# Attention and expert kernel: a head's output and logits in one tile, scratch rows stored by heads, output rows copied from scratch

## The chip, the cores and the metric

One NeuronCore of a Trainium2 chip runs the whole program. The metric is the device time of one execution in microseconds. Engines are named as the profile names them: PE is TensorE's matrix product, PEld its weight load, DVE VectorE, ACT ScalarE, POOL GpSimd and SP SyncE, which computes nothing here and issues nearly all DMAs.

## What is computed

Linear attention over 8 batches of 8 heads, 576 tokens of 64 features, then a mixture of 8 experts over all 4,608 tokens, of which each takes at most one.

```python
def phi(x):
    proj = np.einsum('bhsd,df->bhsf', x, w_phi)                 # 64 -> 128
    proj = proj - np.max(np.abs(proj), axis=-1, keepdims=True)
    return np.concatenate([np.exp(proj), np.exp(-proj)], axis=-1)
kv = np.einsum('bhsf,bhsd->bhfd', k_p, v);  z = np.sum(k_p, axis=2)
x = einsum(q_p, kv) / (einsum(q_p, z) + 1e-06)                  # one row of 512 per token
do_compute = x @ w_skip > 0;  out = x.copy()
logits = x @ w_gate                                             # 8 experts
e_idx = argmax(logits);  gate_w = softmax(logits)[e_idx]
out[do_compute] = x + gate_w * (np.maximum(x @ w1[e], 0.0) @ w2[e])
```

## The kernel before

**Attention.** The work runs in steps. A unit is four heads of one batch, for keys or for queries (16 units of each kind), and has 5 parts: four of 512 rows each (two heads by half of the tokens) and one, part 0, for the last 64 tokens of all heads. Each step takes one part of a key unit and one of a query unit through the stages: load (`st_load`, L287), transpose on VectorE (`st_t`, L324 and L322), projection on PE and two full passes on VectorE (`st_proj`, L347, L354, L357), exponentials on ScalarE, for queries after a transpose on PE (`st_exp_k`, `st_exp_q`, L393), sums on GpSimd (L380) and the attention products on PE (`st_use_k`, L415; `st_use_q`, L513, for the tails L492). The matrix that queries are multiplied by is extended beforehand (L446), so that one product gives 64 output columns, 9 partial logits (8 experts and the skip score) and the denominator: 74 columns a head, four heads or head parts to a PSUM bank.

`norm` (L460) empties that bank on VectorE: denominator (L464), reciprocal (L468), the product for the 64 output columns (L475, into `xm`, or `xt` for the tails of two batches) and the product for the 9 logits (L476, into `lgm` or `lgt`). It runs 72 times: 64 full parts and 8 tails.

`post(b)` (L541) follows a batch's last part: it sums the logits over heads (L568), finds the expert of each token, forms the gate value (`gate`, L592 and L590 write it and the token's number into two columns behind the second half of `xm`), counts places within the experts (`rank`, with masks on GpSimd in L637 and, for batches 0 to 5, four mask instructions in L646 that feed the products of L657), and stores. Three kinds of stores leave on SP's queue: `store_half` (L531, L533) puts the first four heads' columns into `xrows`, a scratch array in DRAM with rows of 514 numbers; `store_rows` (L596, L598) puts the second half with the two extra columns there; `rest` (L668, L673) writes both halves from SBUF to `out`.

**Experts.** After the picks of the first experts (`pick`, L685, `pick_third`) weights stream in by SP in chunks of 512 KB (L184, L187), ScalarE and VectorE or GpSimd split each into a high and a low part (L195, L200), GpSimd gathers token rows from `xrows` by index (L213), PE multiplies (L942 to L961), and GpSimd scatters finished rows over `out` (L889).

**What sets the order.** Every engine runs its own queue in order. From step 8 to 79 the order of PE and ScalarE is the one written in the program; the order of VectorE, GpSimd and SP, and all orders outside those steps up to the experts, is planned when the program is built, from modelled durations and dependences. In the expert part the order is written by hand. Steps in which pieces of `post` are due are given in `later` (gate 2 steps after the batch, `store_rows` 4, `rank` 4, the index products 7, `rest` 7). The last batch does gate and `store_rows` at once; its `rest` is called once eight weight chunks have been asked for (L1206). SP's queue is in order, so a DMA that waits holds the ones behind it.

Of the kernel before, what the change touches and what calls it, by code (L numbers as in the profile page):

```python
# [8 lines left out]
F32 = mybir.dt.float32  # L9
# [9 lines left out]
P = 128  # L19
# [5 lines left out]
def kernel(  # L25
# [17 lines left out]
    SQ = S  # L43
# [76 lines left out]
    const.tile([1, 64], I32, name="spare")  # L120
    mark = const.tile([1, 32], I32, name="mark")[:, 0:1]

    ft = const.tile([P, NSL, 4], I32, name="ft")
# [132 lines left out]
    with actx:  # L256
# [200 lines left out]
                )  # L457
            kva_of[u.g] = kva

        def norm(o, xdst, ldst, shape):  # L460

            den = small.tile([P, 4], F32, tag="den", name="den")
            rec = small.tile([P, 4], F32, tag="rec", name="rec")
            nc.vector.tensor_scalar(  # L464
                out=den.rearrange("p (t o) -> p t o", o=1), in0=o[:, :, NA1:NAUG],
                scalar1=1e-6, scalar2=None, op0=ALU.add,
            )
            nc.vector.reciprocal(out=rec, in_=den)  # L468
            rv = rec.rearrange("p (t o) -> p t o", o=1)
            a, c = shape  # L470

            def sh(x):
                return x.rearrange("p (a c) d -> p a c d", a=a)

            nc.vector.tensor_tensor(out=xdst, in0=sh(o[:, :, 0:D]), in1=sh(rv.broadcast_to([P, 4, D])), op=ALU.mult)  # L475
            nc.vector.tensor_tensor(  # L476
                out=ldst, in0=sh(o[:, :, D:NA1]), in1=sh(rv.broadcast_to([P, 4, NA1 - D])), op=ALU.mult)

        def st_use_q(u, i):
            if i == 0 and u.b % 2 == 0:  # L480
# [4 lines left out]
            if i == 0:  # L485

                for h in range(4):
                    pr, hd = h // 2, h % 2
                    for half in range(2):
                        for par in range(2):  # L490
                            g = u.g - NQ * (1 - par)
                            nc.tensor.matmul(  # L492
                                ov[par * 64:par * 64 + 64, h, :],
                                et_of[g][:, half, hd * P + pr * 64:hd * P + pr * 64 + 64], kva_of[g][:, half, h, :],
                                start=(half == 0), stop=(half == 1),
                            )
                if u.hq == 0:
                    xt_of[u.b // 2] = (
                        [xp.tile([P, 1, 4 * D + 2 * h], F32, tag="xt%d" % h, name="xt") for h in range(2)],
                        xp.tile([P, 1, H, E + 1], F32, tag="lgt", name="lgt"),  # L500
                    )
                xt, lgt = xt_of[u.b // 2]
                norm(ov, xt[u.hq][:, 0, 0:4 * D].rearrange("p (h a d) -> p a h d", h=2, d=D),
                     lgt[:, 0, u.hq * 4:(u.hq + 1) * 4, :].rearrange("p (a h) e -> p a h e", a=2), (2, 2))
# [3 lines left out]
            h0 = u.hq * 4 + 2 * pr  # L508
            for j in range(2):
                for hd in range(2):  # L510
                    for half in range(2):
# [4 lines left out]
                                start=(half == 0), stop=(half == 1),  # L516
                            )
            if u.hq == 0 and i == 1:
                xm_of[u.b] = (
                    [xp.tile([P, 4, 4 * D + 2 * h], F32, tag="xm%d" % h, name="xm") for h in range(2)],  # L520
                    xp.tile([P, 4, H, E + 1], F32, tag="lgm", name="lgm"),
                )
            xm, lgm = xm_of[u.b]
            norm(ov, xm[u.hq][:, 2 * th:2 * th + 2, 0:4 * D].rearrange(
                "p a (h r d) -> p a r h d", h=2, d=D)[:, :, pr],
                 lgm[:, 2 * th:2 * th + 2, h0:h0 + 2, :], (2, 2))
            if i == 4:
                c = slice(0, 4 * D)
# [12 lines left out]
        def post(b):  # L541
            last = b == B - 1
            xs, lgm = xm_of[b]
            xm = xs[1]
            t0 = 9 * (b // 2) + 4 * (b % 2)
            parts = [(xm, lgm, 0, 4)]
            if b % 2 == 1:
                xts, lgt = xt_of[b // 2]
                xt = xts[1]
                parts.append((xt, lgt, 4, 1))  # L550
            nt = 4 if b % 2 == 0 else 5
            T = slice(t0, t0 + nt)

# [13 lines left out]
            for xx, lg, o, n in reversed(parts):  # L567
# [17 lines left out]
            def gate():  # L585
                nc.scalar.activation(out=ex[:, 0:nt], in_=d[:, 0:nt], func=AF.Exp)
                nc.vector.tensor_reduce(out=ss[:, 0:nt], in_=ex[:, 0:nt], axis=AX.X, op=ALU.add)
                nc.vector.tensor_scalar(out=gt[:, 0:nt], in0=ss[:, 0:nt], scalar1=1e-9, scalar2=None, op0=ALU.add)
                for xx, lg, o, n in parts:
                    nc.scalar.activation(  # L590
                        out=xx[:, :, 4 * D + 1:4 * D + 2], in_=sid[:, t0 + o:t0 + o + n].rearrange("p (t o) -> p t o", o=1), func=AF.Copy)
                    nc.vector.reciprocal(out=xx[:, :, 4 * D:4 * D + 1], in_=gt[:, o:o + n].rearrange("p (t o) -> p t o", o=1))  # L592
# [17 lines left out]
            def rank():  # L610
# [31 lines left out]
                    count()  # L642
                if b > EB:
                    return
                for s in range(S):
                    nc.vector.scalar_tensor_tensor(  # L646
                        out=rm4[:, 0:nt, :, s], in0=bc(RKH[:, T], nt, E), scalar=float(s), in1=OH[:, T, :],
                        op0=ALU.is_equal, op1=ALU.mult,
                    )

            def index():
                if b > EB:
# [22 lines left out]
            if last:  # L675
                rests.extend((rank, rest))
# [627 lines left out]
```

## Time and profile before

| | us |
|---|---|
| median of 3 runs | 604.68 |
| lowest, highest | 603.16, 605.82 |
| profiled execution | 607.32 |
| its span, first to last instruction | 605.4 |
| busy in the span: PE | 561.3 |
| PEld | 469.8 |
| VectorE | 498.1 |
| ScalarE | 329.0 |
| GpSimd | 375.4 |

The profile is of one execution, a little slower than the median. An engine's busy time is the union of its instructions' times; PE's is modelled where matmuls overlap, so a busy PE may still not be at its peak. The average over the span mixes stages with different limits: attention runs to about 345 us, the experts from there on. The DMA engines moved 108.33 MB, a mean of 179 GB/s, in 250,233 packets, 192,417 of them under 512 bytes.

### The profile page before, as it was taken

The numbers are of one execution on the slowest core, as the hardware profiler recorded it, in microseconds if no ns is written. First come the engines' busy times: TensorE is split into PE (matmuls) and PEld (weight loads), VectorE is DVE, ScalarE is ACT, GpSimd is POOL, SyncE is SP. The second block draws the span as 40 slices with busy tenths as digits, with TensorE's granted clock in tenths as the row PEclk, the third lists the DMA queues.
The fourth block names the chain that finished last, engine by engine and source line by source line (L and its number), as shares of the span: only waits on it lengthen the run. The fifth ranks groups of instructions, "written<-read, shape, count | busy, mean of one in ns | idle before, by whom it ended". The sixth has DMA issues, their size and how long they took to land. (4 is left out here: it accounts for less than half of the span.)

```text
span 605.4 us, 18715 instructions
## 1 busy us (share of the span) xinstructions
PE 561.3 (93%) x7486; PEld 469.8 (78%) x7486; DVE 498.1 (82%) x1085; ACT 329.0 (54%) x649; POOL 375.4 (62%) x399
## 2 busy tenths in 40 slices
PE   4699999999999999999789799899999998999993
PEld 2477887777877788777667799798998987988892
DVE  5779998999989999899898749866789887867841
ACT  3266665665556555565453544345658665656720
POOL 5465567586675866848665635995567674638021
PEclk9799999999999999999899899899999999999997
DMA  9898898876778657521335297489787688777500
GB/s 158 155 156 166 190 196 181 189 135 138 164 160 189 124 142 180 121 74 46 106 106 184 71 300 268 155 289 310 202 284 227 232 288 297 244 224 261 193 20 30
DMA packets 250233, 108.33 MB, mean 179 GB/s; under 512 B 192417, under 2 KB 235553, under 8 KB 250144
## 3 DMA queue, kind: packets, MB, share of 16 engines
q1 hardware_dynamic: 245632, 97.58, 61.7%
q0 software_dynamic: 3200, 9.45, 4.3%
q8 instruction: 60, 0.98, 0.7%
q10 hardware_dynamic: 1312, 0.08, 0.1%
q14 instruction: 29, 0.24, 0.1%
HBM read 83.86 MB, written 24.02 MB: 178 GB/s over the span
## 5 line engine op out<-in xcount | busy, mean ns | idle before, releaser
L380 POOL TENSOR_TENSOR z<-ek 128x512 f32<-128x512 f32 x64 | 81.1, 1274 | 83.1 <-ACT ek L373 66.0
L200 POOL TENSOR_TENSOR w<-wraw_c,w 128x256 fp32r<-128x256 f32 x108 | 98.8, 947 | 49.6 <-ACT w L195 49.5
L195 ACT ACTIVATE w<-wraw_c 128x1024 fp32r<-128x1024 f32 x96 | 97.8, 1051 | 5.8 <-DMA wraw_c<-in_moe_w_dram 5.8
L200 DVE TENSOR_TENSOR w<-wraw_c,w 128x1024 fp32r<-128x1024 f32 x69 | 91.7, 1344 | 9.4 <-ACT w L195 8.2
L354 DVE TENSOR_REDUCE m<-ps_P 128x8 f32<-128x1024 f32 (+2 forms) x86 | 88.7, 1032 | 2.8 <-PE ps_P L347 2.8
L357 DVE TENSOR_TENSOR u<-ps_P,m 128x1024 f32<-128x1024 f32 (+2 forms) x86 | 88.5, 1029 | 2.3
L347 PE MATMUL ps_P<-wsrc,xT 64*64 64x128 f32 x2048 | 75.2, 283 | 14.2 <-DVE u L357 7.3
L513 PEld LDWEIGHTS ps_O<-kva,eq 128*64 128x64 f32 x2048 | 74.6, 138 | 16.3 <-DVE cs L703 4.7
L513 PE MATMUL ps_O<-kva,eq 128*64 128x74 f32 x2048 | 77.6, 230 | 6.7 <-DVE cs L703 4.1
L399 ACT ACTIVATE eq<-ps_U 128x512 f32<-128x512 f32 x64 | 38.2, 596 | 83.5 <-PE ps_U L393 82.5
L347 PEld LDWEIGHTS ps_P<-wsrc,xT 64*64 64x64 f32 x2048 | 59.5, 138 | 25.8 <-issue 14.7
L415 PE MATMUL ps_K<-ek,v 128*64 128x256 f32 x512 | 70.3, 394 | 0.0
L889 POOL DMA_INDIRECT out_dram<-o,si x22 | 32.4, 1474 | 57.1 <-DVE si L888 50.5
L956 PE MATMUL ps_O<-w,hh 128*128 128x512 f32 x160 | 64.2, 401 | 0.5 <-DVE o L903 0.5
L637 POOL TENSOR_SCALAR OP<-iota_p,rkp,wcol 128x128 bf16<-128x128 f32 x62 | 48.6, 795 | 13.4 <-DVE rec L468 7.2
L324 DVE STREAM_TRANSPOSE xT<-raw 128x512 f32<-128x512 f32 x64 | 43.9, 697 | 8.6 <-PE ps_P L347 4.5
L393 PE MATMUL ps_U<-ident,u 128*128 128x128 f32 x288 | 49.7, 291 | 0.3 <-DVE den L464 0.3
L372 ACT ACTIVATE ek<-u 128x512 f32<-128x512 f32 x64 | 41.0, 641 | 16.5 <-DVE u L357 9.7
L960 PE MATMUL ps_O<-w,hh 128*128 128x512 f32 x120 | 47.4, 395 | 0.1
L961 PE MATMUL ps_O<-w,hlo 128*128 128x512 f32 x120 | 47.3, 394 | 0.0
L415 PEld LDWEIGHTS ps_K<-ek,v 128*64 128x64 f32 x512 | 33.5, 139 | 16.5 <-issue 7.1
L386 POOL TENSOR_TENSOR z<-z,ekt 64x512 f32<-64x512 f32 x32 | 40.8, 1275 | 5.2 <-DMA xg<-xrows,idg 2.9
(254 smaller groups left out, 1203.6 us busy)
## 6 DMA issues: line engine op xcount, KB each, us to landing
wraw_c<-in_moe_w_dram SPq DMA_DIRECT2D x96, 512.0 KB, 5.3
raw<-in_k_dram SPq DMA_DIRECT2D x64, 144.0 KB, 3.2
raw<-in_q_dram SPq DMA_DIRECT2D x64, 144.0 KB, 3.6
v<-in_v_dram SPq DMA_DIRECT2D x64, 128.0 KB, 2.8
out_dram<-xm SPq DMA_DIRECT2D x16, 512.0 KB, 5.2
xrows<-xm SPq DMA_DIRECT2D x8, 516.0 KB, 3.9
xrows<-xm SPq DMA_DIRECT2D x8, 512.0 KB, 4.6
vt<-in_v_dram SPq DMA_DIRECT2D x32, 32.0 KB, 3.5
```

What stands on the lines that cost most here:

```text
L195: nc.scalar.activation(out=hi, in_=raw, func=AF.Copy)
L200: eng.tensor_tensor(out=lo[:, r], in0=raw[:, r], in1=hi[:, r].bitcast(F32), op=ALU.subtract)
L347: nc.tensor.matmul(p[s * 64:s * 64 + 64, hd, (nj + j) * NF:(nj + j + 1) * NF], xT[r, g * P + s * 64:g * P + s * 64 + 64], wsrc[r], start=T ...
L354: nc.vector.tensor_reduce(out=m.rearrange("p (j h) -> p j h", h=2), in_=pv, axis=AX.X, op=ALU.max, apply_absolute_value=True)
L357: nc.vector.tensor_tensor(out=uu[:, 0:2 * nj, :].rearrange("p (j h) f -> p j h f", h=2), in0=pv, in1=m.rearrange("p (j h o) -> p j h o", h ...
L380: zeng.tensor_tensor(out=z, in0=e[:, 0:2, :], in1=e[:, 2:4, :], op=ALU.add)
L393: nc.tensor.transpose(t[:, tt * P:(tt + 1) * P], uu[:, tt, :], ident)
L415: nc.tensor.matmul(o[hd * 64:hd * 64 + 64, :], u.v[:, 2 * hd + pr, g * D:(g + 1) * D], u.e[i][:, 2 * j + hd, :], start=(g == 0), stop=False,)
L513: nc.tensor.matmul(ov[s * 64:s * 64 + 64, 2 * j + hd, :], e[:, half, j, hd, s * 64:s * 64 + 64], kva[:, half, 2 * pr + hd, :], start=(half ...
L637: (nc.vector if last else nc.gpsimd).tensor_scalar(out=OP[:, t0 + t, c, :], in0=iota_p, scalar1=rkp[:, t:t + 1], scalar2=wcol[:, NT:NT + 1 ...
L956: nc.tensor.matmul(y[sub], hh[:, t], wh[:, fi, :], start=first, stop=False)
L960: nc.tensor.matmul(y[sub], hh[:, t], wl[:, fi, :], start=False, stop=False)
```

## The change

The 64 output columns and the 9 logits of a head now lie side by side in one tile: `xm` is [2 halves, 4 row groups, 4 heads, 73], `xt` [2, 1, 4, 73], and `lgm` and `lgt` are gone. `norm` writes both with one product. The sum of the logits reads them out of that tile, over halves and heads at once. Gate value and token number are written over the last head's first two logit columns, after these have been summed. As a head's columns are no longer next to the next head's, `put_x` stores the scratch rows by heads: four DMAs for a half of a batch, each with pieces of 256 bytes, and one for the tail. The second half's x columns are stored without waiting for the gate, whose two columns go out in DMAs of their own (pieces of 8 bytes). The rows of `out` are copied from the scratch array, DRAM to DRAM, in one DMA for a batch and two for a tail. The four mask instructions become two: a comparison of the place's high part with 0 to 3, and a product with the expert mask. `spare`, a tile that nothing reads, shrinks by 128 bytes.

```diff
@@ norm
-            nc.vector.tensor_tensor(out=xdst, in0=sh(o[:, :, 0:D]), in1=sh(rv.broadcast_to([P, 4, D])), op=ALU.mult)
             nc.vector.tensor_tensor(
-                out=ldst, in0=sh(o[:, :, D:NA1]), in1=sh(rv.broadcast_to([P, 4, NA1 - D])), op=ALU.mult)
+                out=dst, in0=sh(o[:, :, 0:NA1]), in1=sh(rv.broadcast_to([P, 4, NA1])), op=ALU.mult)
@@ st_use_q
-            norm(ov, xm[u.hq][:, 2 * th:2 * th + 2, 0:4 * D].rearrange(
-                "p a (h r d) -> p a r h d", h=2, d=D)[:, :, pr],
-                 lgm[:, 2 * th:2 * th + 2, h0:h0 + 2, :], (2, 2))
+            norm(ov, xm[:, u.hq, 2 * th:2 * th + 2].rearrange("p a (h r) d -> p a r h d", h=2)[:, :, pr], (2, 2))
...
                     def store_half(b=u.b, xm=xm):
-                        nc.sync.dma_start(out=rowm[b][:, :, c], in_=xm[0])
-                        if b % 2 == 1:
-                            nc.sync.dma_start(out=rowt[b // 2][:, c], in_=xt_of[b // 2][0][0][:, 0])
+                        put_x(b, 0, xm, xt_of.get(b // 2))
...
+        def put_x(b, h, xm, xt):
+            for a in range(4):
+                c = slice((4 * h + a) * D, (4 * h + a + 1) * D)
+                nc.sync.dma_start(out=rowm[b][:, :, c], in_=xm[:, h, :, a, 0:D])
+            if b % 2 == 1:
+                c = slice(4 * h * D, 4 * (h + 1) * D)
+                nc.sync.dma_start(out=rowt[b // 2][:, c].rearrange("p (n d) -> p n d", d=D), in_=xt[:, h, 0, :, 0:D])
@@ post
-                    out=L[:, o:o + n, :], in_=lg.rearrange("p t h e -> p t e h"), axis=AX.X, op=ALU.add,
+                    out=L[:, o:o + n, :], in_=xx[:, :, :, :, D:NA1].rearrange("p a t h e -> p t e a h"), axis=AX.XY,
+                    op=ALU.add,
...
+            put_x(b, 1, xm, xt)
+
             def store_rows():
-                c = slice(4 * D, XW)
-                nc.sync.dma_start(out=rowm[b][:, :, c], in_=xm)
+                c = slice(DM, XW)
+                nc.sync.dma_start(out=rowm[b][:, :, c], in_=xm[:, 1, :, 3, D:D + 2])
                 if b % 2 == 1:
-                    nc.sync.dma_start(out=rowt[b // 2][:, c], in_=xt[:, 0])
+                    nc.sync.dma_start(out=rowt[b // 2][:, c], in_=xt[:, 1, 0, 3, D:D + 2])
@@ rank
-                for s in range(S):
-                    nc.vector.scalar_tensor_tensor(
-                        out=rm4[:, 0:nt, :, s], in0=bc(RKH[:, T], nt, E), scalar=float(s), in1=OH[:, T, :],
-                        op0=ALU.is_equal, op1=ALU.mult,
-                    )
+                eqs = sm("eqs", [5, S], BF16)
+                nc.vector.tensor_tensor(
+                    out=eqs[:, 0:nt], in0=iota_p[:, 0:S].rearrange("p (o s) -> p o s", o=1).broadcast_to([P, nt, S]),
+                    in1=bc(RKH[:, T], nt, S), op=ALU.is_equal)
+                nc.vector.tensor_tensor(
+                    out=rm4[:, 0:nt], in0=OH[:, T, :].rearrange("p t (e o) -> p t e o", o=1).broadcast_to([P, nt, E, S]),
+                    in1=eqs[:, 0:nt].rearrange("p t (o s) -> p t o s", o=1).broadcast_to([P, nt, E, S]), op=ALU.mult)
@@ rest
-                for h in range(2):
-                    c = slice(h * 4 * D, (h + 1) * 4 * D)
-                    nc.sync.dma_start(
-                        out=out[b * SQ:b * SQ + 4 * P, c].rearrange("(g p) m -> p g m", p=P), in_=xs[h][:, :, 0:4 * D])
-                    if b % 2 == 1:
-                        for par in range(2):
-                            o = (b - 1 + par) * SQ + 4 * P
-                            nc.sync.dma_start(out=out[o:o + 64, c], in_=xts[h][par * 64:par * 64 + 64, 0, 0:4 * D])
+                nc.sync.dma_start(out=out[b * SQ:b * SQ + 4 * P], in_=xr[b // 2, b % 2 * 4 * P:(b % 2 + 1) * 4 * P, 0:DM])
+                if b % 2 == 1:
+                    for par in range(2):
+                        o, r = (b - 1 + par) * SQ + 4 * P, 8 * P + par * 64
+                        nc.sync.dma_start(out=out[o:o + 64], in_=xr[b // 2, r:r + 64, 0:DM])
```

## Rows read from the trace of the kernel before

**Rows 1.** Busy time of each engine in four stretches. The columns: the stretch in us from the span's start, its length, then busy us (and instructions) of PE, PEld, DVE, ACT and POOL, the granted TensorE clock, the DMA engines' mean busy share and GB/s.

```profile
60.00:120.00 60.00, 58.41 (x1187) 47.81 (x1185) 56.81 (x141) 36.26 (x87) 38.00 (x34) 1.00 0.89 191
120.00:285.00 165.00, 159.16 (x3159) 128.01 (x3154) 156.59 (x386) 97.93 (x235) 117.61 (x111) 1.00 0.61 136
285.00:345.00 60.00, 51.35 (x869) 39.02 (x868) 51.50 (x155) 28.91 (x60) 38.49 (x39) 0.95 0.35 109
...
345.00:600.00 255.00, 245.89 (x1554) 221.00 (x1552) 188.33 (x328) 137.20 (x206) 147.75 (x162) 0.98 0.69 229
```

**Rows 2.** What PE waited for from 30 to 285 us, all of it: who waited, for whom, then us in total, times, and the longest in us.

```profile
PE ps_O L513 <- ACT kva L454: 2.3, 7, 0.3
PE ps_O L657 <- DVE den L464: 1.9, 3, 0.7
PE ps_O L657 <- POOL OP L637: 1.1, 2, 0.6
PE ps_P L347 <- DVE u L357: 1.1, 3, 0.4
PE ps_O L492 <- ACT kva L454: 0.9, 3, 0.3
```

**Rows 3.** What VectorE waited for from 30 to 285 us, all of it, in the same columns.

```profile
DVE xT L324 <- PE ps_P L347: 3.9, 9, 1.2
DVE den L464 <- PE ps_O L513: 3.8, 7, 1.3
DVE m L354 <- PE ps_P L347: 0.9, 2, 0.5
DVE acc L663 <- PE ps_O L657: 0.9, 2, 0.5
DVE acc L661 <- PE ps_O L657: 0.5, 1, 0.5
```

**Rows 4.** What PE waited for from 285 to 345 us, all of it.

```profile
PE ps_O L513 <- DVE cs L703: 4.1, 2, 3.1
PE ps_U L816 <- DVE x L820: 1.6, 1, 1.6
PE ps_P L942 <- ACT x L819: 1.4, 1, 1.4
PE ps_O L657 <- POOL OP L637: 0.6, 1, 0.6
PE ps_O L446 <- DVE lgm L476: 0.4, 1, 0.4
PE ps_U L393 <- DVE den L464: 0.3, 1, 0.3
```

**Rows 5.** Groups of instructions by line over the whole span: line, engine, operation, out<-in, out<-in as partitions x elements, count, then busy us and mean ns of one, and idle us before them.

```profile
L475 DVE TENSOR_TENSOR xm<-ps_O,rec 128x256 f32<-128x256 f32 x64 | 27.1, 423 | 1.9
...
L476 DVE TENSOR_TENSOR lgm<-ps_O,rec 128x36 f32<-128x36 f32 x64 | 11.8, 184 | 0.0
...
L568 DVE TENSOR_REDUCE L<-lgm 128x36 f32<-128x288 f32 x8 | 5.4, 674 | 0.2
```

**Rows 6.** Instructions of VectorE in order of time: start us, us, engine, line, operation. The last row is of four instructions that follow one another, from the start of the first to the end of the last.

```profile
68.47 0.43 DVE L475 TENSOR_TENSOR xm<-ps_O,rec 128x256 f32<-128x256 f32 x1
68.82 0.18 DVE L476 TENSOR_TENSOR lgm<-ps_O,rec 128x36 f32<-128x36 f32 x1
68.92 0.15 DVE L464 TENSOR_SCALAR den<-ps_O 128x4 f32<-128x4 f32 x1
...
200.68 0.68 DVE L646 SCALAR_TENSOR_TENSOR rm<-RKH,OH 128x40 bf16<-128x40 int32 x4
```

**Rows 7.** SP's DMA queue in two short stretches that hold little else than one kind of transfer: packets, MB, and the time the packets took as a share of 16 engines over the stretch. The first is of 258.5 to 264 us (5.5 us), where v is loaded in pieces of 256 bytes; the second of 329.8 to 335 us (5.2 us), where one half of a batch is stored in pieces of 1 KB.

```profile
q1 hardware_dynamic: 2243, 0.55, 44.6%
...
q1 hardware_dynamic: 528, 0.52, 29.1%
```

**Rows 8.** A load of the ninth key unit as SP issues it (four DMAs), that unit's first transpose on VectorE, and the longest of SP's own waits from 30 to 285 us (in the columns of rows 2).

```profile
90.71 3.75 SPq L293 DMA_DIRECT2D raw<-in_k_dram  x4
...
133.97 0.29 DVE L322 STREAM_TRANSPOSE xTt<-raw 128x128 f32<-128x128 f32 x1
...
SPq L301 <- PE ps_K L415: 31.7, 9, 6.1
```

**Rows 9.** Where the expert part begins: SP's issues in order of time, the split of two weight chunks on GpSimd (in brackets what it waited for before) and the product on PE that first reads it, the bytes moved from 350 to 355 us (in the columns of rows 1), and the last batch's store as a row of the DMA issues from 348 to 370 us (count, KB, us to landing).

```profile
347.84 0.41 SPq L596 DMA_DIRECT2D xrows<-xm  x1
...
353.83 1.82 SPq L673 DMA_DIRECT2D out_dram<-xt  x2
356.81 0.39 SPq L184 DMA_DIRECT2D wraw_c<-in_moe_w_dram  x1
...
363.35 5.63 POOL L200 TENSOR_TENSOR w<-wraw_c,w 128x256 fp32r<-128x256 f32 x8 [2.92 <-ACT w L195]
...
370.91 0.64 PE L945 MATMUL ps_P<-x,w 128*128 128x256 f32 x4
...
350.00:355.00 5.00, 5.00 (x44) 5.00 (x43) 1.65 (x3) 3.09 (x4) 2.84 (x4) 1.00 1.04 340
...
xrows<-xm SPq DMA_DIRECT2D x1, 516.0 KB, 6.0
```

**Rows 10.** Batch 3: the output store of the second half's x columns as SP issues it, and the instruction that writes the gate column beside them.

```profile
187.87 0.91 SPq L668 DMA_DIRECT2D out_dram<-xm  x1
...
193.95 0.18 DVE L592 RECIPROCAL xm<-gt 128x4 f32<-128x4 f32 x1
```

More of the change, by code (lines that the diff above doesn't have):

```diff
@@ L119 @@
     pad0 = const.tile([P, 3, 2], I32, name="pad0")
-    const.tile([1, 64], I32, name="spare")
+    const.tile([1, 32], I32, name="spare")
     mark = const.tile([1, 32], I32, name="mark")[:, 0:1]
@@ L458, in st_aug, with norm @@
             kva_of[u.g] = kva
-        def norm(o, xdst, ldst, shape):
+        def norm(o, dst, shape):
             den = small.tile([P, 4], F32, tag="den", name="den")
@@ L497, in st_use_q @@
                 if u.hq == 0:
-                    xt_of[u.b // 2] = (
-                        [xp.tile([P, 1, 4 * D + 2 * h], F32, tag="xt%d" % h, name="xt") for h in range(2)],
-                        xp.tile([P, 1, H, E + 1], F32, tag="lgt", name="lgt"),
-                    )
-                xt, lgt = xt_of[u.b // 2]
-                norm(ov, xt[u.hq][:, 0, 0:4 * D].rearrange("p (h a d) -> p a h d", h=2, d=D),
-                     lgt[:, 0, u.hq * 4:(u.hq + 1) * 4, :].rearrange("p (a h) e -> p a h e", a=2), (2, 2))
+                    xt_of[u.b // 2] = xp.tile([P, 2, 1, 4, NA1], F32, tag="xt", name="xt")
+                norm(ov, xt_of[u.b // 2][:, u.hq, 0].rearrange("p (h a) d -> p a h d", h=2), (2, 2))
                 return
@@ L507, in st_use_q @@
             e = u.e[i].rearrange("p a (j h c) -> p a j h c", j=2, h=2)
-            h0 = u.hq * 4 + 2 * pr
             for j in range(2):
@@ L518, in st_use_q @@
             if u.hq == 0 and i == 1:
[L519 to L523, printed above, removed]
-            norm(ov, xm[u.hq][:, 2 * th:2 * th + 2, 0:4 * D].rearrange(
-                "p a (h r d) -> p a r h d", h=2, d=D)[:, :, pr],
-                 lgm[:, 2 * th:2 * th + 2, h0:h0 + 2, :], (2, 2))
+                xm_of[u.b] = xp.tile([P, 2, 4, 4, NA1], F32, tag="xm", name="xm")
+            xm = xm_of[u.b]
+            norm(ov, xm[:, u.hq, 2 * th:2 * th + 2].rearrange("p a (h r) d -> p a r h d", h=2)[:, :, pr], (2, 2))
             if i == 4:
-                c = slice(0, 4 * D)
                 if u.hq == 0:
                     def store_half(b=u.b, xm=xm):
-                        nc.sync.dma_start(out=rowm[b][:, :, c], in_=xm[0])
-                        if b % 2 == 1:
-                            nc.sync.dma_start(out=rowt[b // 2][:, c], in_=xt_of[b // 2][0][0][:, 0])
+                        put_x(b, 0, xm, xt_of.get(b // 2))
                     later.append((now[0] + 2, store_half))
@@ L539, in sm @@
             return small.tile([P] + shape, dt, tag=tag, name=tag, bufs=bufs)
+        def put_x(b, h, xm, xt):
[5 more added lines that the diff above has]
+                nc.sync.dma_start(out=rowt[b // 2][:, c].rearrange("p (n d) -> p n d", d=D), in_=xt[:, h, 0, :, 0:D])
         def post(b):
             last = b == B - 1
-            xs, lgm = xm_of[b]
-            xm = xs[1]
+            xm = xm_of[b]
             t0 = 9 * (b // 2) + 4 * (b % 2)
-            parts = [(xm, lgm, 0, 4)]
+            xt = xt_of.get(b // 2)
+            parts = [(xm, 0, 4)]
             if b % 2 == 1:
-                xts, lgt = xt_of[b // 2]
-                xt = xts[1]
-                parts.append((xt, lgt, 4, 1))
+                parts.append((xt, 4, 1))
             nt = 4 if b % 2 == 0 else 5
@@ L565, in bc @@
                 return a.rearrange("p (t o) -> p t o", o=1).broadcast_to([P, n, w])
-            for xx, lg, o, n in reversed(parts):
+            for xx, o, n in reversed(parts):
                 nc.vector.tensor_reduce(
-                    out=L[:, o:o + n, :], in_=lg.rearrange("p t h e -> p t e h"), axis=AX.X, op=ALU.add,
+                    out=L[:, o:o + n, :], in_=xx[:, :, :, :, D:NA1].rearrange("p a t h e -> p t e a h"), axis=AX.XY,
+                    op=ALU.add,
                 )
@@ L588, in gate @@
                 nc.vector.tensor_scalar(out=gt[:, 0:nt], in0=ss[:, 0:nt], scalar1=1e-9, scalar2=None, op0=ALU.add)
-                for xx, lg, o, n in parts:
+                for xx, o, n in parts:
                     nc.scalar.activation(
-                        out=xx[:, :, 4 * D + 1:4 * D + 2], in_=sid[:, t0 + o:t0 + o + n].rearrange("p (t o) -> p t o", o=1), func=AF.Copy)
-                    nc.vector.reciprocal(out=xx[:, :, 4 * D:4 * D + 1], in_=gt[:, o:o + n].rearrange("p (t o) -> p t o", o=1))
+                        out=xx[:, 1, :, 3, D + 1:D + 2], in_=sid[:, t0 + o:t0 + o + n].rearrange("p (t o) -> p t o", o=1), func=AF.Copy)
+                    nc.vector.reciprocal(out=xx[:, 1, :, 3, D:D + 1], in_=gt[:, o:o + n].rearrange("p (t o) -> p t o", o=1))
+            put_x(b, 1, xm, xt)
             def store_rows():
-                c = slice(4 * D, XW)
-                nc.sync.dma_start(out=rowm[b][:, :, c], in_=xm)
+                c = slice(DM, XW)
+                nc.sync.dma_start(out=rowm[b][:, :, c], in_=xm[:, 1, :, 3, D:D + 2])
                 if b % 2 == 1:
-                    nc.sync.dma_start(out=rowt[b // 2][:, c], in_=xt[:, 0])
+                    nc.sync.dma_start(out=rowt[b // 2][:, c], in_=xt[:, 1, 0, 3, D:D + 2])
             if last:
```

1 line of the change is left out of this document (removed).

## The prediction

> **What bounds the kernel now.** I read the busy time by stretches first [rows 1]. The attention part runs to about 345 us, and in its steady stretches two engines are nearly full at once: PE 58.41 of 60 us and then 159.16 of 165 us (97 and 96%), VectorE 56.81 and 156.59 us (95%). From 285 to 345 us, where attention hands over to the experts, both fall to some 51.4 of 60 us. From 345 us on PE is busy 245.89 of 255 us, and VectorE, at 188.33 us, is not what limits there. So the change, which takes work from VectorE, can act only ahead of 345 us, and the question is which of the two full engines sets the pace. The waits answer it. PE waits in all 7.3 us between 30 and 285 us [rows 2], of which only 1.9 and 1.1 us are put down to VectorE (the denominator of L464, the features of L357); the rest is ScalarE's (3.2) and GpSimd's (1.1). VectorE waits 10.0 us in the same stretch [rows 3], 8.6 of it named to PE's projection and attention products, and none of it for a DMA. VectorE thus waits for PE more than PE for VectorE, and PE sets the pace by a small margin. In the handover PE waits 8.4 us [rows 4]: 4.1 for the chain that picks an expert (L703), 1.6, 0.4 and 0.3 for other VectorE work, 2.0 for ScalarE and GpSimd.
>
> **One product for both.** 72 instructions of the small product go (64 for full tiles, 8 for the tails), 184 ns each, and 72 products of 256 columns at 423 ns become 292 columns [rows 5]. Between the two shapes lie 220 columns and 239 ns, 1.09 ns a column, so the long one grows by 39 ns. By durations the relief is 72 x (184 - 39) ns = 10.4 us. But instructions overlap: the small product begins at 68.82 us and the next instruction at 68.92 [rows 6], so it holds the queue for 0.10 us, and the relief by starts is 72 x (100 - 39) ns = 4.4 us. I take 5, near the second, since what follows does not depend on the small product in most places. The reduction of the logits keeps its count of elements (288 at 674 ns, 8 times, and a short one 4 times) and reads them at a wider step; no row shows that, and I take 0, with -1 to +5.4 us (the eight taking twice as long) as bounds.
>
> **Masks in two steps.** Four instructions in a row took 0.68 us [rows 6], in 6 blocks. In their place come a compare of at most 20 elements, no dearer than the 36-column product (0.18), and a product of at most 160 elements, by the slope above 0.145 + 160 x 0.00109 = 0.32 us. That saves 0.18 us a block, 1.1 us in all; bounds 0 and 2 (the product as cheap as the 36-column one). VectorE is relieved by about 6 us, with bounds -1 and 13.
>
> **How much of the 6 us reaches the end.** PE is next late for itself: what VectorE can give back is at most the waits put down to it. The picking chain holds no changed instruction, so 3.0 us in the steady part and 2.3 us in the handover are within reach, 5.3 us. VectorE's busy work from 60 to 345 us is 264.9 us by rows 1, and 6 us is 2% of that; but the waits within reach are made of pieces of under 2 us, at which a norm that is some 0.06 us shorter each time is ahead by several norms' worth. I take 2 us, bounds 0 and 5.3.
>
> **Stores by heads.** A token's row, stored before as two pieces of some 1 KB (9,216 packets), goes out as 8 pieces of 256 bytes (36,864), and the gate value and row number as 4,608 packets of 8 bytes. A 1 KB store cost 0.291 x 5.2 us x 16 engines / 528 = 45.9 ns of one engine, a 256-byte load 0.446 x 5.5 x 16 / 2,243 = 17.5 ns [rows 7]. No row shows a store this small, so its price lies between 17.5 ns (as a load) and 45.9 (as a 1 KB store). At the first, x pieces take 40.3 us of all 16 engines against 26.4 now, and the 8-byte pieces 5.0: 18.9 us more. At the second, 105.8 and 13.2: 92.6 us more. I take 25 us, near the first, as the price of a packet falls with its size between the two rows. Free DMA time from 60 to 345 us, by the DMA shares of rows 1, is 6.6 + 64.4 + 39.0 = 110 us, so even the upper bound has room. Before 120 us it has not, and loads would run late there, by at most some 20 us (four half-batch stores at 4.4 us more each, and their tails). Their lead covers that: the load issued at 90.71 us is first read at 133.97 [rows 8]. Cost 0; without that lead it would be the 19 us.
>
> The rows stop at 256 bytes loaded and 1 KB stored [rows 7]. The Trainium skill, page "DMA: Bandwidth & Descriptors" (Specifications), speaks against this part: it puts the least transfer at full rate at 512 bytes, and has smaller ones read, changed and written back. No run here shows it. As an estimate by that page a 256-byte store is two passes, 35 ns, the five x stores of the last batch take 5.6 us of the engines in place of 2.8, and the second rival's delay of 5 us becomes 7.8, 3.1 past its point of decision, for 607.8 us in place of 602.7.
>
> **Output copied from scratch.** 9,216 packets of 1 KB out of SBUF become 4,608 of 2 KB from DRAM to DRAM. Priced at twice 45.9 ns, that is the same time; bounds are the same and double (each byte passing the memory twice). SP issues 56 stores before and 100 after; 44 at 0.41 us (the store at 347.84 [rows 9]) is 18 us of its queue, at 0.91 (half of the pair at 353.83) 40 us. In the steady part SP waits 31.7 us for PE to free one buffer alone [rows 8], so this is hidden. New is a wait: a copy on SP's queue must wait until all stores of its rows have landed, and the loads queued behind it wait too, 4 to 6 us at worst for each batch [rows 9]. Up to 285 us the lead of some 40 us covers it. The gate's writes lie beside columns that the stores read; in batch 3 the store of the x columns was issued at 187.87 us, before the neighbouring gate column was written at 193.95 [rows 10], so neighbouring columns don't make one wait for another here, and I add no wait on VectorE.
>
> **The sum.** The profiled execution took 607.32 us, a span of 605.4 and 1.9 around it. Less 2 us it gives 605.3. The median of the runs, 604.68, lies 2.64 us below the profiled one, and I carry that over: **602.7 us**.
>
> **Rivals.** *VectorE sets the pace after all* (faster): PE's matmul ends are modelled, and if part of its busy time is waiting, the relief arrives whole, 6 to 12 us, say 9: 595.7 us. For it speaks that VectorE is at 95%; against it, rows 2 and 3.
>
> *The last batch's copy holds up the weights* (slower). At 347.84 us the last scratch rows are stored, output stores follow up to 355.65, and at 356.81 the weight loads go on [rows 9]. After the change the copy waits for the scratch stores. If the last batch's five x stores are issued only then, the queue needs 5 x 0.41 us, they land 6.0 us later, at about 356, the three copies are issued by 358, and their 1.31 MB run ahead of the next weights for 3.9 us at 340 GB/s. The weights come some 5 us late; 9 if DRAM to DRAM moves at half the rate, and 9 as well if small stores cost the upper 45.9 ns (2,560 packets in 7.3 us, not 2.8). The part of them needed first was split from 363.35 us on in two lots of 2.8, so by 366.2, and PE reads it at 370.91: 4.7 us of slack. PE loses up to 4.5 us, so 604.68 + 4.5 = 609.2 us. It decides from a delay of 4.7 us on. Against it speaks that the x columns of the last batch are done before its gate, and can be stored several us before 347.84.
>
> *The planner's order shifts.* The orders of VectorE, GpSimd and SP are planned with durations that change here, and in the handover PE stands idle 8.65 of 60 us, so another order there may cost or give some 6 us: 597 to 609, either sign.
>
> **How the numbers follow.** A measurement of this kernel can tell 0.5%, 3 us, from no change. Forecast (within 3 us, at 602.7): 0.46. VectorE's relief whole: 0.24. The late copy: 0.14 (0.08 by a slow copy, 0.06 by dear small stores). A shifted order: 0.16, of it 0.06 faster and 0.10 slower. So faster 0.30, same 0.46, slower 0.24. The range goes from 595.5 (the first rival's middle) to 610 (just above the second): beyond them I leave about 0.2.
>
> **What would show it.** Right: VectorE's busy time ahead of 345 us down by 5 to 12 us and PE's unchanged, the period of a batch shorter by 0.1 to 0.4 us, DMA share from 120 to 285 us up from 0.61 to about 0.7, and no engine waiting for a load. Wrong: the merged product above 0.50 us; a VectorE or ScalarE instruction of the gate waiting for a store; PE's waits for VectorE gone and the span shorter by over 6 us (first rival); PE waiting near 371 us for a split of weights that landed late (second).

## The result and the profile after

The changed kernel took 610.55 us (median of 22 runs, 605.04 to 613.91), the kernel before 604.89 in the same set (22 runs, 602.27 to 607.02): a ratio of 1.0080, with an interval of 1.0062 to 1.0099. The forecast was 602.7 us, range 595.5 to 610.0. Its runs lie on two levels: 9 of 22 at 605.0 to 607.3 us, 13 at 609.7 to 613.9. The first profile (612.49 us, span 610.5) is of the upper level; a second one (run e7 below: 603.90 us, span 601.9) is of the lower. The two profiles of one program show best where the time went.

The first profile of the changed kernel by stretches, in the columns of [rows 1]:

```profile
60.00:120.00 60.00, 58.84 (x1174) 47.61 (x1172) 56.87 (x126) 36.32 (x87) 38.19 (x34) 1.00 0.81 141
120.00:285.00 165.00, 158.68 (x3143) 128.03 (x3144) 155.11 (x339) 97.89 (x232) 117.09 (x111) 1.00 0.82 147
285.00:300.00 15.00, 11.89 (x202) 8.93 (x202) 13.17 (x32) 7.26 (x15) 9.54 (x8) 0.89 0.90 147
300.00:315.00 15.00, 8.00 (x121) 5.59 (x121) 5.78 (x22) 2.93 (x7) 6.93 (x6) 0.68 0.58 48
...
345.00:360.00 15.00, 11.36 (x90) 10.75 (x91) 9.37 (x23) 7.71 (x12) 9.98 (x13) 0.77 0.72 163
```

Up to 285 us PE and VectorE are as busy as before [rows 1]; only the DMA share has risen, from 0.61 to 0.82 in the long stretch. The loss stands in one place: from 300 to 315 us PE is busy 8.00 of 15 us, where the kernel before has 13.33:

```profile
300.00:315.00 15.00, 13.33 (x230) 9.87 (x227) 14.45 (x37) 8.00 (x21) 9.51 (x8) 1.00 0.26 83
```

What waited in the first profile from 285 to 345 us (columns of [rows 2]):

```profile
DVE den L464 <- PE ps_O L506: 11.8, 6, 8.5
...
POOL z L386 <- DMA xg<-xrows,idg: 7.6, 1, 7.6
...
PE ps_O L433 <- POOL z L386: 7.0, 1, 7.0
...
POOL xg L213 <- DMA xrows<-xm: 5.0, 1, 5.0
```

Read from the bottom: GpSimd's first gather of scratch rows (L213, batches 0 to 5) waits 5.0 us for a scratch store; then GpSimd waits 7.6 us for that gather; the sums z of the attention part stand behind both on GpSimd's queue, PE waits 7.0 us for them, and VectorE waits 8.5 for PE. In the kernel before the gather did not wait for a store but for its indices, and PE's waits here were those of [rows 4], none for z:

```profile
296.18 1.21 POOL L213 DMA_INDIRECT xg<-xrows,idg  x1 [1.13 <-DVE idg L222]
```

Why the store was late, on SP's queue (start us, us, engine, line, what):

```profile
285.54 1.09 SPq L529 DMA_DIRECT2D xrows<-xm  x2
290.17 0.55 SPq L662 DMA_DIRECT2D out_dram<-xrows  x1
290.82 0.56 SPq L590 DMA_DIRECT2D xrows<-xm  x1
291.48 0.44 SPq L592 DMA_DIRECT2D xrows<-xt  x1
```

L590 and L592 store the gate and row number of batch 5. They stand behind the copy L662, which waits until the x pieces of 285.54 have landed. The kernel before stored batch 5's last rows some 19 us sooner:

```profile
271.66 0.37 SPq L596 DMA_DIRECT2D xrows<-xm  x1
272.13 0.45 SPq L598 DMA_DIRECT2D xrows<-xt  x1
```

The same lines in the second profile:

```profile
278.90 0.55 SPq L662 DMA_DIRECT2D out_dram<-xrows  x1
279.55 0.56 SPq L590 DMA_DIRECT2D xrows<-xm  x1
280.21 0.44 SPq L592 DMA_DIRECT2D xrows<-xt  x1
```

The order is the same, 11.3 us earlier, and in this execution the store is in time. GpSimd in the first and then in the second profile:

```profile
298.53 1.21 POOL L213 DMA_INDIRECT xg<-xrows,idg  x1 [4.96 <-DMA xrows<-xm]
300.04 0.95 POOL L213 DMA_INDIRECT xg<-xrows,idg  x1 [0.30 <-issue]
308.63 1.25 POOL L386 TENSOR_TENSOR z<-z,ekt 64x512 f32<-64x512 f32 x1 [7.64 <-DMA xg<-xrows,idg]
```

```profile
294.07 1.21 POOL L213 DMA_INDIRECT xg<-xrows,idg  x1 [1.13 <-DVE pad L223]
295.58 0.95 POOL L213 DMA_INDIRECT xg<-xrows,idg  x1 [0.30 <-issue]
300.91 1.29 POOL L386 TENSOR_TENSOR z<-z,ekt 64x512 f32<-64x512 f32 x1 [4.37 <-PE ps_O L433]
```

The late store is not the whole of the delay. The gather starts 4.5 us later than in the second profile (298.53 against 294.07 us), and its two parts then take 8.9 us from issue to landing, against 4.5 in the second profile and 3.7 in the kernel before (DMA issues from 299 to 309 us of the first profile: count, us to landing):

```profile
xg<-xrows,idg POOLq DMA_INDIRECT x2, 8.9
```

The copy of 290.17 us and six x pieces of batch 6, issued from 292.02 us on, go out just ahead of it; in the second profile that copy went out 11.3 us sooner. No run separates what the late store and the slow landing cost each.

And PE, again first and second:

```profile
309.94 1.07 PE L433 MATMUL ps_O<-z,ones_f 128*32 128x256 f32 x4 [7.00 <-POOL z L386]
310.94 0.90 PE L393 MATMUL ps_U<-ident,u 128*128 128x128 f32 x3
311.77 2.24 PE L506 MATMUL ps_O<-kva,eq 128*64 128x74 f32 x32
```

```profile
302.25 0.62 PE L433 MATMUL ps_O<-z,ones_f 128*32 128x256 f32 x4 [1.50 <-POOL z L386]
302.81 0.55 PE L393 MATMUL ps_U<-ident,u 128*128 128x128 f32 x3
303.29 1.25 PE L506 MATMUL ps_O<-kva,eq 128*64 128x74 f32 x32
```

The wait costs 5.5 us more (7.00 against 1.50), and the same matmuls then take nearly twice as long (2.24 against 1.25 us): after the idle time the granted clock stood at 0.50 from 306 to 315 us, its lower level (1.2 of 2.4 GHz), where in the second profile it stayed at 1.00 (first and second, columns of [rows 1]):

```profile
306.00:315.00 9.00, 5.06 (x52) 3.55 (x56) 0.84 (x4) 0.87 (x2) 5.98 (x5) 0.50 0.08 15
```

```profile
300.00:315.00 15.00, 13.50 (x179) 8.93 (x173) 13.54 (x28) 7.49 (x20) 13.17 (x11) 1.00 0.43 106
```

At 309.94 us PE is 7.7 us behind the second profile's 302.25. Of these, 2.2 us were lost before the wait: PE stops 3.1 us for the picking chain in both profiles, but from 295 to 300 us the granted clock was 0.66 in the first (0.69 in the kernel before) and 1.00 in the second, so some 2 us of the second profile's lead are not of this mechanism. By the end of the handover the gap has grown: the second product of the expert part (L936) starts 9.6 us later, at 352.98 against 343.37 us. The spans differ by 8.6 us.

### The profile page after: what moved, and what is told of

It reads as the page before. It is cut to its first block, busy times and chain, and to the rows that moved or that the text cites. A ratio compares the mean times of both kernels' runs of the same rounds, so it can differ in the third digit from the quotient of the medians.

```text
span 610.5 us, 18713 instructions
## 1 busy us (share of the span) xinstructions
PE 562.0 (92%) x7486; PEld 470.3 (77%) x7486; DVE 493.1 (81%) x1001; ACT 328.8 (54%) x649; POOL 373.3 (61%) x399
## 3 DMA queue, kind: packets, MB, share of 16 engines
q1 hardware_dynamic: 273984, 97.58, 69.1%
## 5 line engine op out<-in xcount | busy, mean ns | idle before, releaser
L347 PE MATMUL ps_P<-wsrc,xT 64*64 64x128 f32 x2048 | 76.7, 288 | 14.1 <-DVE xT L324 7.2
L506 PEld LDWEIGHTS ps_O<-kva,eq 128*64 128x64 f32 x2048 | 74.9, 138 | 16.4 <-ACT kva L454 4.2
L347 PEld LDWEIGHTS ps_P<-wsrc,xT 64*64 64x64 f32 x2048 | 60.8, 141 | 25.8 <-issue 14.6
```

What stands on the lines that cost most here:

```text
L347: nc.tensor.matmul(p[s * 64:s * 64 + 64, hd, (nj + j) * NF:(nj + j + 1) * NF], xT[r, g * P + s * 64:g * P + s * 64 + 64], wsrc[r], start=T ...
L506: nc.tensor.matmul(ov[s * 64:s * 64 + 64, 2 * j + hd, :], e[:, half, j, hd, s * 64:s * 64 + 64], kva[:, half, 2 * pr + hd, :], start=(half ...
```

## The experiments

Edits first, each against the kernel named, cut to the core. The expectations name their theories by letters: A, the order on SP's queue makes the loss; A2, that order together with a queue that is behind; B, the DMA time of the small pieces; C, a copy in flight slows every other DMA; D, a copy in flight makes the first gather land late; E, the two levels have nothing to do with that copy.

e1, on the changed kernel, for every batch but the last (`gst[b]` is its last gate store):

```
+    with tc.issue_after(gst[b].ins):
         rest()                      # the copies
```

> The changed kernel with one order on SP's queue: each batch's copy is issued behind that batch's own gate and row-number pieces instead of ahead of them. Theory A (queue order: the last pieces of batch 5 stand behind its waiting copy, the first gather waits for them, GpSimd's queue and then TensorE wait): the gather's 5.0 us wait for the scratch stores falls below 1.5 us, TensorE's 7.0 us wait for the z of GpSimd falls below 4, the time to 604 to 607 us. Rival B (the DMA time of the 256-byte and 8-byte pieces): unchanged, 609 to 612. Rival C (the copy in flight slows every other DMA): the wait for the stores may go, but the gather still takes 8 to 9 us to land and the time stays at 608 to 611.

e2, on the kernel before: each 1 KB store of x as in the changed kernel's put_x, gate columns alone.

```
-    nc.sync.dma_start(out=rowm[b][:, :, c], in_=xm)
+    put_x(b, 1, xm, xt)
+    nc.sync.dma_start(out=rowm[b][:, :, DM:XW], in_=xm[:, :, 4 * D:4 * D + 2])
```

> The kernel before with one part of the change: scratch rows stored by heads in 256-byte pieces, gate and row number in 8-byte pieces of their own; output rows still from SBUF in 1 KB rows, products and masks as before. A: no copy is there to stand in the way, 604 to 606.5 us, the gather waits under 1.5 us for stores. B: most of the loss, 608 to 612. C: as before, 604 to 606.

e3, on the kernel before: `rest` is that of the changed kernel.

> The kernel before with one part of the change: output rows copied from scratch; scratch rows stored as before (1 KB and 1032 B with gate and row number, so the copy can only follow them), products and masks as before. A: 603 to 606.5 us. B: 603 to 606. C: 607 to 611, and the stretch in which a copy runs shows DMA packets several times as long as before.

e4, on the changed kernel: three pieces of the second half stored at once, the fourth with the gate.

```
-    c = slice(DM, XW)
-    nc.sync.dma_start(out=rowm[b][:, :, c], in_=xm[:, 1, :, 3, D:D + 2])
+    c = slice(DM - D, XW)
+    nc.sync.dma_start(out=rowm[b][:, :, c], in_=xm[:, 1, :, 3, 0:D + 2])
```

> The changed kernel without the 8-byte pieces: gate and row number are stored with the last head's piece (264 B), which waits for the gate; a copy then follows it by itself. A: as e1, 604 to 607 us. B: if it is the 8-byte pieces, 604 to 607 with the DMA share of 120 to 300 us lower by a fifth or more; if it is the 256-byte pieces, 609 to 612. C: 608 to 611.

e5, on e4: batch 5's `rest` is called in batch 6's, under `tc.issue_after` of batch 6's gate store.

> The kernel of e4 with batch 5's copy moved behind batch 6's last piece on SP's queue, so that no copy is in flight when the first gathers read. Of e4's runs 7 lay at 603.8 to 605.6 us and 3 at 608.3 to 611.0, with a lower mean clock. Theory D (a copy in flight makes the first gather land late in some executions, TensorE idles, the clock falls): no run above 607, median 603.5 to 605. Rival E (the two levels have nothing to do with that copy): 2 to 4 of 10 runs stay at 608 to 611, median as e4's, 605 to 606.

e6, on e4: `rest` does nothing, so the rows of `out` that no expert writes stay unwritten.

> The kernel of e4 with the copies of output rows left out for all batches (rows of out that no expert writes stay unwritten): the most that copies can cost. D: no run above 607, median 602 to 604.5. E: 605 to 606 with some runs at 608 to 611. If DVE's relief is worth what the start of the expert stage shows (344.1 us in e4, 345.5 in the kernel before), the median is 1 to 2 us below the kernel before, 602.5 to 603.5.

e7 is the changed kernel; its profile fell on the lower level, with the signs that theory A gave for it.

> The changed kernel once more, for a second profile: its runs lie at 605 to 607 us or at 610 to 614. If this profile is of the lower group, theory A expects the first gather to wait less or to land sooner (TensorE's wait on z below 4 us instead of 7.0, granted clock of 300 to 315 us above 0.9); if of the upper, the same picture as in the first. Rival E: the same waits in both groups.

e8, on the kernel before: the loop of four masks replaced by the changed kernel's compare and product; e10 is the same kernel again.

> The kernel before with one part of the change: masks in two steps. The prediction's 1.1 us less of VectorE before 285 us, of which at most 1 us reaches the end: 603.5 to 605.5, no difference that can be measured. Rival (the planner's order shifts with it): over 2 us either way, with PE's waits in other places.

> The kernel of e8 (before, with masks in two steps) in more rounds: its ratio was 0.998 with an interval that holds 1. Theory: 1 us less, 0.9975 to 0.9995, interval below 1 or just at it. Rival (noise): 1.000 or more.

e9, on e4: as e5, for batches 0 to 5.

> The kernel of e4 with the copies of batches 0 to 5 all moved behind batch 6's last piece (they go out from some 318 us on). Theory A2 (the output rows on top of the pieces fill the DMA engines from 60 to 260 us, SP's queue falls 10 to 20 us behind, and only so do batch 5's last rows come late): SP issues the load of k that stands at 245.4 us in the changed kernel at 219 to 224, as without copies, batch 5's last pieces at 269 to 272, and no run of the upper level before 315 us; the whole at 603.5 to 605.5 unless six copies in a row hold back the expert weights, which would show as a wait of ScalarE's w for wraw at 330 to 350 us and add 3 to 10 us. Rival (the queue is slow because of the number of pieces alone): load of k at 235 to 245 as in e4, gate pieces at 277 to 282.

e11, on e3: x stored without the gate columns, these under `tc.issue_after` of the copy. e12, on e2: e3's copies, and the gate stores under `tc.issue_after` of the copy.

> The kernel before with the changed kernel's order on SP's queue but not its 256-byte pieces: x rows stored in 1 KB rows, output rows copied from scratch, the gate and row-number pieces (8 B) behind the copy. Theory A2 (two conditions: the queue is behind by 10 to 20 us, and the last pieces stand behind the copy): the order alone does nothing, batch 5's last pieces at 274 to 280 us, the gather waits under 0.5 us for them, 604 to 606.5. Rival (the order is enough by itself): the gather waits 2 us or more and the time is 607 to 611.

> The kernel before with the changed kernel's whole transport and nothing of its VectorE part: scratch rows in 256-byte pieces, output rows copied from scratch, gate and row-number pieces (8 B) behind the copy; products and masks as before. Theory A2 (a queue that is behind and the order together make the loss, VectorE's part has no share in it): median 607 to 611, runs on two levels, the upper in a third or more of them, SP's load of k that stands at 222.5 us before at 232 to 248, batch 5's last pieces at 279 to 292. Rival (the loss needs the changed norm, logits or masks, or the order that they give the other engines): 604 to 606.5, one level.

What was measured. Ratio with its interval; runs above 608.4 us, a mark chosen after the runs (no run of the kernel before, 118 in all sets, was slower than 608.37); then from each profile the start in us of SP's last load of k, of batch 5's last scratch store, of the first gather (in brackets a wait put down to stores), and of the second expert product on PE.

| kernel | median us | ratio | above 608.4 | load of k | last store | gather | expert |
|---|---|---|---|---|---|---|---|
| before | 604.89 | 1 | 0 of 118 | 222.49 | 272.13 | 296.18 | 345.48 |
| changed | 610.55 | 1.0062 to 1.0099 | 13 of 22 | 245.40 | 291.48 | 298.53 (4.96) | 352.98 |
| e7 changed, again | 603.90 (one run) | | 0 of 1 | 234.69 | 280.21 | 294.07 | 343.37 |
| e1 copy behind gate | 607.50 | 1.0015 to 1.0065 | 3 of 10 | 241.79 | 282.26 | 298.03 (1.13) | 347.71 |
| e2 pieces alone | 605.07 | 0.9996 to 1.0040 | 1 of 10 | 238.27 | 277.66 | 295.29 | 345.33 |
| e3 copy alone | 606.47 | 1.0000 to 1.0038 | 0 of 10 | 222.80 | 272.42 | 296.46 | 345.67 |
| e4 gate with head 7 | 605.56 | 1.0005 to 1.0062 | 3 of 10 | 241.41 | 280.25 | 293.96 (1.13) | 344.11 |
| e5 batch 5's copy late | 605.44 | 0.9982 to 1.0033 | 1 of 10 | 231.19 | 269.89 | 293.81 | 344.68 |
| e6 no copies | 604.11 | 0.9972 to 0.9997 | 0 of 10 | 220.56 | 269.62 | 293.51 | 343.67 |
| e8 masks alone | 604.23 | 0.9957 to 1.0008 | 0 of 10 | 220.97 | 270.40 | 294.38 | 343.65 |
| e9 all copies late | 622.09 | 1.0264 to 1.0340 | 4 of 4 | 222.24 | 271.11 | 295.00 | 358.93 |
| e10 masks again | 604.08 | 0.9967 to 1.0000 | 0 of 12 | 221.88 | 271.30 | 295.28 | 344.46 |
| e11 order alone | 604.89 | 0.9980 to 1.0015 | 0 of 10 | 222.18 | 271.79 | 295.79 | 344.84 |
| e12 both conditions | 607.44 | 1.0006 to 1.0053 | 3 of 12 | 236.39 | 280.62 | 295.13 | 344.21 |

*The queue.* The load column splits the kernels in two. With pieces of 256 bytes and output rows both in the attention part (changed, e1, e2, e4, e5, e7, e12) SP issues its loads 9 to 23 us later than before; without one of the two (e3, e6, e8 to e11) it does not. PE waits for no load in any of these traces between 30 and 345 us, VectorE for 0.4 us at most (e4, e9), so for these two engines the lead of the loads covers the lag, as forecast; ScalarE has one wait of 3.5 us put down to a load of v, in e12. But scratch stores are issued by the same queue, and batch 5's last ones move with it, from 272 to 278 to 291 us.

*The order.* e1 and e4 put the gate pieces ahead of the copy or into the last x piece: the gather's wait is 1.13 us, which is what it waits for its indices in the other kernels, PE's wait for z is gone, and the ratio falls to 1.004 and 1.0034: about half of the loss, with intervals that just touch the changed kernel's. With batch 5's copy moved away as well nothing measurable is left: e5 has 1.0007, though with one run at 610.81, which theory D excluded; e6 has no such run. e11 has the order without the lag, and the gather finds its rows: 0.9997. So the order alone does nothing, and in kernels whose queue is not behind no run of 52 (e3, e6, e8, e10, e11) was above 608.4 us.

*Two kinds of upper run.* Of the changed kernel's 13 runs on the upper level ten have a mean granted clock of 0.972 to 0.976 (the profiled one 0.974; the kernel before has 0.975 to 0.987 in all sets that list it), and three 0.980 or 0.981, as the nine on the lower level have (0.978 to 0.982). So the picture of the first profile, with its fallen clock, need not stand for all 13. In e1 no run is of the first kind: its three runs above 608.4 have 0.979 to 0.981. But in e4 two of three (0.972, 0.974), and e5's one (0.974), still have the low mean clock, though their profiles, of lower runs, show no gather waiting for a late store. What those runs waited for was not profiled.

*Pieces, copies and DMA time.* e2 adds 44 us of all 16 engines (69.3% of 602.7 us against 61.7% of 605.4) and is not measurably slower: theory B falls. e3 moves the output by copies at 61.9% of 606.4 us, 2 us more than before, with a ratio of 1.0000 to 1.0038: copies beside 1 KB stores cost no more than 0.4%. That does not test theory C beside 256-byte pieces, and there the slow landing of the first profile (8.9 us) speaks for it; the last section has the prices.

*Too late is worse.* e9 takes the copies of batches 0 to 5 out of the attention part. Queue and stores are on time, as theory A2 said, but from 314 us on the copies run ahead of the last batch's rows and of the weights. PE's wait and ScalarE's from 315 to 400 us, and a stretch in the columns of [rows 1]:

```profile
PE ps_P L947 <- ACT x L824: 17.5, 1, 17.5
```

```profile
ACT w L195 <- DMA xrows<-xm: 16.7, 1, 16.7
ACT w L195 <- DMA wraw_c<-in_moe_w_dram: 12.9, 7, 5.9
```

```profile
345.00:360.00 15.00, 3.01 (x14) 3.01 (x15) 2.33 (x7) 5.73 (x10) 5.37 (x8) 0.50 1.12 184
```

I had allowed 3 to 10 us for this; it cost 17.

*What did not come out.* e12 has the changed kernel's transport in full; the expectation was 607 to 611 with the upper level in a third of the runs or more. It came to 607.44 with 3 of 12, one of them at 608.42, just above the mark, and its profile is of a lower run. Two runs of 610.88 and 611.92 us show that transport alone can make upper runs, but it does not make all of the loss: the intervals, 1.0006 to 1.0053 and 1.0062 to 1.0099, do not meet. What the changed products and masks, or the order that they bring, add to it stays open. In e12's profile no store is late, and yet the gather takes 4.9 us to land, GpSimd waits for it, and PE then waits 2.2 us for z:

```profile
302.65 1.25 POOL L386 TENSOR_TENSOR z<-z,ekt 64x512 f32<-64x512 f32 x1 [5.06 <-DMA xg<-xrows,idg]
```

Open, too, is e1, where 3 of 10 runs are above 608.4 although its profile, itself of such a run (608.59 us), shows no late gather; that profile has one stop of PE of 2.59 us, ending at 178.63 us, put down to nothing.

## Why the prediction was wrong

**The step that failed** is the one on the copies: "the loads queued behind it wait too, 4 to 6 us at worst for each batch", covered by "the lead of some 40 us". The wait is as forecast (4.6 us from the x pieces at 285.54 to the copy at 290.17), and the loads' lead does cover it. But the list of what is queued behind the copy was short by one: the gate and row-number stores of the same batch. Batch 5's have a reader with a date, the first gather near 294 us. In the kernel before they led it by 19 us (issued at 272.13, landed after a median of 4.9, read at 296.18). The queue's lag and the copy's wait together moved them by 8 us in e7, which the lead still covered, and by 19 in the first profile, with 5 of it the copy's; there the lead was gone, the more so as the gather comes due some 2 us sooner (294.07 us in e7 against 296.18). Little slack is left behind the gather: PE waits 1.5 us for z even in e7, and in the first profile 7.0, with the lower clock after it. The second thing left out is that the copy and the pieces behind it then run beside the gather, which lands in 8.9 us instead of 3.7. The first profile shows both steps directly; that they make the loss of every upper run is not shown.

**Stores by heads** were put at 25 us of DMA time, bounds 18.9 and 92.6; the changed kernel shows 48 us more in the first profile (69.1% of 610.5 us) and 33 in the second (67.6% of 601.9). The price of a piece was right where pieces run alone: in this row of SP's queue of the first profile, from 344 to 350 us,

```profile
q1 hardware_dynamic: 2113, 0.52, 39.3%
```

it is 0.393 x 6 x 16 / 2,113 = 17.9 ns, and the working took 17.5 [rows 7] for its lower end. The Trainium skill's rule on stores under 512 bytes ("DMA: Bandwidth & Descriptors", Specifications), by which the prediction made 35 ns of it, does not show in this row; the load that gave the 17.5 is as short, so what both bear would not show either. The increase lies above the 25 us all the same: without output rows it is some 20 us (e6: 368 us, where 374 less the 26 worked out for 9,216 packets of 1 KB would leave 348), with them up to 48 (last section). Cost 0 for the DMA time held as such (e2); that a fuller queue also issues its stores later was not worked out.

**One product for both**: 0.462 us was worked out, and the changed kernel shows 461 ns; the logit reduction is 665 against 674 ns. Masks: 0.50 us a block worked out for the two steps, 0.46 to 0.49 measured. The rows of VectorE from 30 to 345 us of the first profile, in the columns of [rows 5]:

```profile
L475 DVE TENSOR_TENSOR xm<-ps_O,rec 128x292 f32<-128x292 f32 x62 | 28.6, 461 | 2.1
L559 DVE TENSOR_REDUCE L<-xm 128x36 f32<-128x288 f32 x7 | 4.7, 665 | 0.2
...
L643 DVE TENSOR_TENSOR rm<-OH,eqs 128x160 bf16<-128x160 bf16 x3 | 0.9, 314 | 0.0
L643 DVE TENSOR_TENSOR rm<-OH,eqs 128x128 bf16<-128x128 bf16 x3 | 0.8, 282 | 0.0
L640 DVE TENSOR_TENSOR eqs<-iota_p,RKH 128x20 bf16<-128x20 f32 x3 | 0.5, 180 | 0.0
L640 DVE TENSOR_TENSOR eqs<-iota_p,RKH 128x16 bf16<-128x16 f32 x3 | 0.5, 176 | 0.0
```

VectorE is busy 493.1 us in place of 498.1, 5.0 less, where some 6 were taken; the second profile has 3.6 less, e4 to e6 between 2.7 and 4.8. **How much reaches the end**: 2 us were taken, bounds 0 and 5.3. From batch 0's to batch 5's routing (the maximum of its logits) the kernel before takes 194.35 us, the changed kernel 194.2 in both profiles, e4 to e6 193.3 to 193.6, and masks alone 193.5: the merged product adds nothing there that shows, which fits a pace set by PE. In the handover batch 7's routing comes 78.3 us after batch 5's before and 74.9 to 75.8 in e7, e4 and e6, but the expert part starts only 1.4 to 2.1 us sooner; PE then waits 2.8 us for ScalarE's x where it waited 1.4 [rows 4]. In the medians no more than 1 us is left: 604.11 without copies, 604.08 with the masks alone.

**Signs.** Right as named were the period of a batch in e4 to e6 (0.15 to 0.2 us shorter), though not in the changed kernel itself, and no engine waited for a load in its two profiles from 30 to 345 us; the DMA share from 120 to 285 us went to 0.82, not to 0.7, and VectorE's busy time from 60 to 345 us fell by 2.2 us in e7 (262.7 against 264.9), not by 5 to 12. No gate instruction waits for a store in the changed kernel. But [rows 10] did not show that neighbouring columns never do so, only that one store did not wait for a later write, and in e2 ScalarE's write of the token number waits 1.2 us, put down to a scratch store.

**Rivals.** VectorE does not set the pace. The last batch's copy did not hold up PE: in e7 it is issued at 346.83 us, the next weights at 352.21 (356.81 before [rows 9]), and no wait of PE for weights there is above 0.7; with seven batches' copies ahead of the weights the mechanism is real (e9). (Its 4.5 us is 4.3 by its own terms, 9 less 4.7.) A planner's shift was the nearest of the three, but it was given as a lump with no place; the place was one order on one queue.

## What to carry to other kernels

When a wait is put on a queue, list everything that is issued behind it with its reader and that reader's date, stores as well as loads: the loads' lead says nothing about a store. DMA time that is hidden for the loads still moves the whole queue, and the first thing with a date to fall out was small here (4 KB). If a program's runs lie on two levels, profile it until both have been seen, and compare the two before anything else.

The best kernel here is the one before with the masks in two steps: 604.08 us, 0.9967 to 1.0000 of its time, a gain at the edge of what can be measured. It has none of the rest of the change.

## What was not expected of the hardware

Small pieces are cheap alone and dear behind a copy. They cost 17.9 ns of one engine in the row above. In the first profile, from 296 to 298 us, x pieces go out right behind the copy of 290.17 us; then, from 299 to 309 us, they do so with the gather on GpSimd's queue:

```profile
q1 hardware_dynamic: 982, 0.24, 155.0%
```

```profile
q1 hardware_dynamic: 1073, 0.26, 63.6%
q0 software_dynamic: 160, 0.53, 38.6%
```

1.55 x 2 x 16 / 982 = 50 ns for each piece, when none of the gather's packets was yet in flight, and 0.636 x 10 x 16 / 1,073 = 95 ns beside the gather, whose own packets (3.3 KB in the mean) take 386 ns each. In the second profile, from 295 to 301 us, about as many pieces run beside the same gather with no copy just ahead of them:

```profile
q0 software_dynamic: 160, 0.53, 36.7%
q1 hardware_dynamic: 1056, 0.26, 20.0%
```

There a piece takes 18 ns and a packet of the gather 220. So the gather's company does not make pieces dear. Behind a copy and without a gather they take 35 ns in e7 (286 to 288 us), 48 in e1 and 67 in e4 (292 to 294 us), and 17 in e6, which has no copies (285 to 287 us). That a copy ahead of them goes with a high price is shown in these traces; why is not.

Busy shares do not add either: pieces without output rows (e6) take 368 us of all 16 engines, less than the kernel before with 1 KB stores and output rows (374), while either form of the output rows on top of them brings it to between 407 us (e7) and 442 (e1); e2, whose output rows are 1 KB stores and no copies, has 418.

The same program's queue drifted apart by 11 us between two executions (load of k at 234.69 and 245.40 us); what sets the drift is open.
